# Linear attention and a GELU network on one core: a table of shifts for the order, and three changes of who does what

## The chip, the cores and the metric

The kernel runs on one core of a Trainium2 chip. The metric is the device time of one execution in microseconds (us). Before the change three executions took 814.27 us in the median (813.37 to 816.61). The engines are TensorE (PE in the rows, with PEld for its weight loads), VectorE (DVE), ScalarE (ACT), GpSimd (POOL) and SyncE (SP); DMA transfers are issued by SyncE and GpSimd.

## The reference

q, k and v have 8 batches, 8 heads, 576 positions and 64 channels. The network has 4608 tokens (8 x 576), 512 channels in and out and 2048 hidden ones.

```python
q_s = exp(q - max(q, axis=-1)); q_s = q_s / (sum(q_s, axis=-1) + 1e-9)
k_s = exp(k - max(k, axis=2));  k_s = k_s / (sum(k_s, axis=2) + 1e-9)
kv = einsum('bhsd,bhse->bhde', k_s, v)
x = einsum('bhsd,bhde->bhse', q_s, kv).transpose(0, 2, 1, 3).reshape(4608, 512)
h = x @ w_in
out = (h * (1.0 / (1.0 + exp(-1.702 * h)))) @ w_out
```

So q is normalised over its channels, k over the positions, and each is 64 wide.

## The kernel before

The 4608 tokens are nine blocks t = 0 to 8 of 512. For each block the attention gives x (512 channels by 512 tokens), and the network runs over it in eight steps, each with a pair of 128-wide slices of the hidden layer. The weights arrive as pairs of 32-bit words (float64); `conv` turns them, on ScalarE (L349, L391) and VectorE (L354, L358, L394), into a high and a low part, and every product of the network is taken in three matmuls: high by high, high by low, low by high.

Block 0 multiplies plainly: `plain1` (L895) and `ffn2` (L1200), matmuls of 512 columns. From block 1 the first product, and from block 3 the second as well, is done on half blocks in seven products in place of eight (`ffn1`, `ffn2s`, all through `matmul`, L316, 256 columns, in sixes). These need sums of the weight quarters: `sums` makes those of `w_in` during block 1 (VectorE L462 to L475 and, last, L486 into a tile `wt`, of which there are two), and `sums2` those of `w_out` during block 2 (VectorE L510 to L526, ScalarE L531). The weights and sums go to DRAM (`kept`, `kept_t`, `kept_u`) and are loaded again for every later block, by GpSimd (L426, and `load_u` at L1015).

`sums2` works with two buffers of 4 KB a partition: the finest part `fine` lies in the second half of the tile X (even steps) or in O (odd steps), the rounded part `split` always in the first half of X. Both are stored by SyncE (L529) into interleaved rows: each partition writes four pieces of 1 KB, and `load_u` reads rows of 2 KB.

The attention of block t runs beside the network of block t - 1. For k: maximum over the positions (VectorE, then an all-reduce on GpSimd, L638), subtraction (VectorE L649, L652), exponential (ScalarE L655, L656), and `kv_pairs` on TensorE (L728). For the first batch the subtraction of k is done by TensorE instead (`k_sub_first`, L675 to L680: identity times k plus minus one times the maximum), for all four pairs of heads (hp 0 to 3). For q: `q_soft` takes the maximum (L759), subtracts (L760), takes the exponential on ScalarE (L763), sums (L766), adds 1e-9 (L767), inverts (L768) and multiplies (L769), in one instruction each for a tile of 512 elements a partition; `q_tr` transposes a pair of heads by four small matmuls (L784) and copies them from PSUM (L788); `x_pairs` (L806) multiplies by kv.

After each stretch of such other work on TensorE, `again()` sets a counter: the next BACK matmuls of 256 columns run with their columns reversed, and the STEPS = 4 after them in another permutation. Until the first real work TensorE runs fills on zeros (L302).

The order is not written out by hand. `Plan.add` lists every operation with engine, cost in us, what it reads and writes, and a rank. `due()` goes over TensorE's operations in rank order, adds up their costs and works backwards to the time by which each operation must be done. `forward()` then plays the program: on every engine that is free it starts, among the operations whose inputs are there, the one due first. TABLE is a cost for changing ScalarE's function table, LAND and RATE are costs of a transfer. `order()` gives the instructions of each engine in the order in which the play began them, and they are issued so.

## Time and profile before

| what | value |
|---|---|
| median of three executions | 814.27 us (813.37 to 816.61) |
| the profiled execution | 812.7 us, span 810.9 us, so 1.8 us outside the span |
| TensorE busy | 800.1 us, 99% of the span, 6652 matmuls |
| of these, matmuls of 256 columns at L316 | 4704 (784 sixes) |
| VectorE, ScalarE, GpSimd busy | 679.1, 588.2, 255.9 us |
| granted clock of TensorE | 0.999 of 2.4 GHz |
| DMA | 204.08 MB; SyncE's queue 31.3%, GpSimd's 52.9% of 16 engines |

The span is the time from the first to the last instruction in the trace; the execution's own time is a little longer. A busy share is an average over the whole run. In the order of time, VectorE is nearly full in the first 200 us and has room later. A view in order of time gives the start of a group of like instructions, the time from its first start to its last end, and in brackets idle time ahead of it and who ended it. Matmuls overlap, so that the next group may start before this time is over.

### The profile page before, as it was taken

How to read it: one execution, taken by the hardware profiler on the slowest of the kernel's cores; microseconds unless marked ns; L12 is line 12 of the kernel's file. 1: busy time of each engine (PE TensorE's matmuls, PEld its weight loads, DVE VectorE, ACT ScalarE, POOL GpSimd, SP SyncE). 2: the span in 40 equal slices, each digit the busy share in tenths (PEclk: the TensorE clock that was granted, in tenths of full speed). 3: DMA queues.
4: the chain of work that ended last, by engine and by line, in shares of the span. 5: the costliest groups of instructions: out<-in, count | busy, mean ns of one | idle time of the engine just before them, and what ended most of it. 6: DMA issues, size and time to landing. Idle time of an engine off the chain costs nothing.

```text
span 810.9 us, 17790 instructions
## 1 busy us (share of the span) xinstructions
PE 800.1 (99%) x6652; PEld 736.8 (91%) x6652; DVE 679.1 (84%) x1300; ACT 588.2 (73%) x1136; POOL 255.9 (32%) x439
## 2 busy tenths in 40 slices
PE   9999999999999999999999999999999999999997
PEld 4777789988898879999999999999999999999997
DVE  8999999999869975889779988899889975686557
ACT  5798886887947866896768895899697845565442
POOL 1120202122222442544244423453343234333530
PEclk9999999999999999999999999999999999999999
DMA  9999766776299968997599868986897589768973
GB/s 286 352 355 325 253 234 221 217 246 214 82 331 283 361 204 239 323 317 226 171 272 353 250 183 241 347 275 181 242 298 217 155 246 291 221 170 245 312 229 100
DMA packets 119478, 204.08 MB, mean 252 GB/s; under 512 B 18656, under 2 KB 64224, under 8 KB 118368
## 3 DMA queue, kind: packets, MB, share of 16 engines
q0 software_dynamic: 53856, 123.23, 52.9%
q1 hardware_dynamic: 65536, 79.71, 31.3%
q8 instruction: 53, 0.87, 0.5%
q14 instruction: 33, 0.27, 0.1%
HBM read 168.30 MB, written 34.60 MB: 250 GB/s over the span
## 4 chain that ended last, share of the span: by engine, by line
PE 87%; DMA 6%; DVE 5%; issue 2%; POOL 0%; ACT 0%; SPq 0%; DVEq 0%; POOLq 0%
PE bank L316 64%; PE bank L1200 11%; PE bank L895 3%; PE bank L728 2%; PE bank L806 2%; DMA kept_u<-O 2%; PE bank L784 2%; DMA vl<-in_v 1%; DMA raw<-in_moe_w_out 1%; DMA wj<-kept 1%; DMA raw<-in_moe_w_in 1%; PE bank L302 1%; DMA qT<-in_v 1%; PE bank L675 0%; DVE xo L874 0%
## 5 line engine op out<-in xcount | busy, mean ns | idle before, releaser
L316 PE MATMUL bank<-xo,wt 128*128 128x256 f32 x1536 | 219.4, 278 | 0.5 <-DVE X L964 0.4
L316 PEld LDWEIGHTS bank<-xo,wt 128*128 128x128 f32 x1536 | 198.4, 188 | 9.1 <-issue 1.4
L316 PE MATMUL bank<-xo,wj 128*128 128x256 f32 x1152 | 167.2, 281 | 1.8 <-DVE X L964 1.7
L316 PEld LDWEIGHTS bank<-xo,wj 128*128 128x128 f32 x1152 | 146.8, 188 | 6.4 <-ACT X L970 2.8
L426 POOL DMA_DIRECT2D wj<-kept x138 | 73.2, 531 | 214.9 <-PE bank L316 184.1
L316 PE MATMUL bank<-w,gh 128*128 128x256 f32 x1008 | 140.0, 277 | 0.2
L316 PE MATMUL bank<-w,gl 128*128 128x256 f32 x1008 | 139.2, 277 | 0.0
L964 DVE TENSOR_TENSOR X<-bank,X 128x256 f32<-128x256 f32 x192 | 79.7, 419 | 65.3 <-PE bank L316 53.3
L316 PEld LDWEIGHTS bank<-w,gh 128*128 128x128 f32 x1008 | 126.3, 188 | 0.7 <-issue 0.3
L316 PEld LDWEIGHTS bank<-w,gl 128*128 128x128 f32 x1008 | 126.2, 188 | 0.0
L1200 PE MATMUL bank<-w,gh 128*128 128x512 f32 x384 | 119.8, 393 | 0.8 <-DVE w L394 0.8
L1015 POOL DMA_DIRECT2D w<-kept_u x152 | 80.5, 530 | 119.4 <-PE bank L316 91.5
L960 ACT COPY X<-bank 128x256 f32<-128x256 f32 x192 | 70.1, 370 | 62.4 <-PE bank L316 60.1
L970 ACT ACTIVATE X<-X 128x256 f32<-128x256 f32 x192 | 77.7, 415 | 51.9 <-DVE X L964 51.0
L1124 DVE TENSOR_TENSOR O<-bank,O 128x512 f32<-128x512 f32 x101 | 69.0, 684 | 11.1 <-PE bank L316 10.7
L1200 PEld LDWEIGHTS bank<-w,gh 128*128 128x128 f32 x384 | 66.9, 188 | 12.5 <-DVE w L394 1.3
L1200 PE MATMUL bank<-w,gl 128*128 128x512 f32 x192 | 75.5, 393 | 0.1
L426 POOL DMA_DIRECT2D wt<-kept_t x84 | 44.5, 530 | 83.0 <-PE bank L316 69.3
L1051 DVE TENSOR_TENSOR X<-X 128x512 f32<-128x512 f32 x96 | 66.5, 699 | 4.4 <-ACT X L970 3.2
L638 POOL PARTITION_ALL_REDUCE mx<-mx x32 | 36.7, 1147 | 98.0 <-DVE mx L634 94.6
L1062 DVE TENSOR_TENSOR gh<-X,gh 128x512 fp32r<-128x512 f32 x84 | 57.3, 683 | 8.4 <-ACT gh L1066 8.2
L1062 DVE TENSOR_TENSOR gl<-X,gl 128x512 fp32r<-128x512 f32 x84 | 57.3, 684 | 3.6 <-ACT gl L1066 3.4
(130 smaller groups left out, 1192.1 us busy)
## 6 DMA issues: line engine op xcount, KB each, us to landing
wt<-kept_t POOLq DMA_DIRECT2D x84, 512.0 KB, 5.9
w<-kept_u POOLq DMA_DIRECT2D x152, 256.0 KB, 5.6
wj<-kept POOLq DMA_DIRECT2D x126, 256.0 KB, 5.2
kt<-in_k SPq DMA_DIRECT2D x32, 256.0 KB, 7.0
raw<-in_moe_w_in SPq DMA_DIRECT2D x16, 512.0 KB, 8.4
raw<-in_moe_w_out SPq DMA_DIRECT2D x16, 512.0 KB, 6.6
kept<-wj SPq DMA_DIRECT2D x16, 512.0 KB, 5.7
kept_t<-wt SPq DMA_DIRECT2D x8, 1024.0 KB, 5.0
```

Source lines behind the costliest of these rows:

```text
L316: nc.tensor.matmul(out, w, x, skip_group_check=True, **flags)
L426: "POOL", 0.6, (key,), to, R(t, step - 2, off), lambda: nc.gpsimd.dma_start(out=out(), in_=src), size=size
L638: nc.gpsimd.partition_all_reduce(flat, flat, P, bass_isa.ReduceOp.max)
L895: nc.tensor.matmul(bank[bk], w[:, c // 2, l, c % 2 * P : (c % 2 + 1) * P], x[:, r], start=c == 0 and e == 0, stop=c == KC - 1 and e == 2)
L960: vec("ACT", act(HT), (("bank", bk),), (A(n),), slot, lambda: nc.scalar.copy(a(n), ph[bk]))
L964: nc.vector.tensor_tensor(out=a(n), in0=ph[bk], in1=a(n), op=ALU.add)
L970: vec("ACT", act(HT), K, (A(n),), slot, lambda: nc.scalar.activation(a(n), x, AF.Gelu_apprx_sigmoid), "gelu")
L1015: nc.gpsimd.dma_start(out=wo[s, 0][:, 1].rearrange("p s f -> p (s f)"), in_=kept_u[p][:, c * DM : (c + 1) * DM])
L1051: nc.vector.tensor_tensor(out=x[:, :, o], in0=x[:, :, n], in1=x[:, :, m], op=op)
L1062: nc.vector.tensor_tensor(out=L[s][:, 1], in0=x[:, :, src], in1=L[s][:, 0].bitcast(F32), op=ALU.subtract)
L1124: nc.vector.tensor_tensor(out=half(u, to), in0=bv(b), in1=o, op=ALU.add)
L1200: nc.tensor.matmul(bank[c].rearrange("p (d f) -> p d f", d=2), l, r, start=first_ and e == 0, stop=last and e == 2)
```

## The change

Four things change.

1. The order. A table MOVES of 1535 whole numbers, of which 1263 are not zero, is added, in tenths of a microsecond, to the due times before `forward()` plays the program. The play's constants change: LAND 1.8 to 3.2, RATE 340e3 to 320e3, a TensorE stop of over 1 us after 35 us costs 1.5 more, consecutive instructions overlap by 0.1 us on ScalarE and 0.08 on VectorE, the units of the network on TensorE cost 0.69.
2. First k and q. Of the first k, head pairs 2 and 3 are subtracted by VectorE and go to ScalarE as in later batches; pairs 0 and 1 stay on TensorE. For q of block 0 the maximum is taken negated, and ScalarE takes eight exponentials per tile, each of 64 elements with the maximum as its bias and its sum as a second output (`accum_out`); VectorE's subtraction and its sum go.
3. Transposes. From block 1 `q_tr` does two pairs of head pairs in one run, eight matmuls into two banks. BACK is 5 in place of 6.
4. Sums of `w_out`. In odd steps both parts lie in O; in even steps in X. Each part is stored in one row of 4 KB a partition, and `load_u` reads two pieces of 1 KB.

```diff
--- before.py
+++ after.py
@@ -16,6 +16,57 @@
 AX = mybir.AxisListType
 
 
+MOVES = """
+305 60 -68 -35 0 -21 -48 -501 -1307 -8 -258 14 12 22 44 -23 5 60 -5 -401 45 -45 275 -139 -314 -265 355 -297 20 19 -110
...
+"""
+
+
 class Plan:
 
 
@@ -24,11 +75,13 @@
 
 
 
-    HOP, LAND, RATE, ISSUE = 0.1, 1.8, 340e3, 0.5
+    HOP, LAND, RATE, ISSUE = 0.1, 3.2, 320e3, 0.5
     AHEAD = 6.0
+    STALL = 1.5
 
     WARM = 27.0
     TABLE = {"ACT": 1.28, "POOL": 7.0}
+    OVERLAP = {"ACT": 0.1, "DVE": 0.08}
 
     def __init__(self):
         self.ops, self.fill = [], None
@@ -94,7 +147,10 @@
                 _, cost, _, _, _, needs, size, late = ops[n]
                 if needs is not None and needs != table.get(e):
                     cost, table[e] = cost + self.TABLE[e], needs
-                free[e] = done = now + cost
+                if e == "PE" and now > 35.0 and now - free[e] > 1.0:
+                    cost += self.STALL
+                done = now + cost
+                free[e] = done - self.OVERLAP.get(e, 0.0)
                 if size:
                     wire = max(wire, done) + size / self.RATE
                     done = wire + self.LAND + late
@@ -116,12 +172,16 @@
                 now = min(times)
         return began, start, end
 
+    def moved(self, due):
+        moves = [0.1 * int(x) for x in MOVES.split()]
+        return [min(d, 1e6) + (moves[n] if n < len(moves) else 0.0) for n, d in enumerate(due)]
+
     def order(self):
         self.users = [[] for _ in self.ops]
         for n, o in enumerate(self.ops):
             for d in o[2]:
                 self.users[d].append(n)
-        began, self.start, self.end = self.forward(self.due())
+        began, self.start, self.end = self.forward(self.moved(self.due()))
         return began
 
 
@@ -210,6 +270,7 @@
     mx = [sb(f"mx{i}", [P, 2, D]) for i in range(NP)]
     m1 = sb("m1", [P, 2, 2, D])
     qm = [sb(f"qm{i}", [P, 2 * C]) for i in range(2)]
+    qs_ = [X[1][:, 1, 0, 8 * i : 8 * i + 8] for i in range(2)]
     r_ = sb("r", [P, 2, NP])
     rs = [r_[:, i] for i in range(2)]
     kl, vl = sb("kl", [P, H, D]), sb("vl", [P, H, W])
@@ -303,7 +364,7 @@
 
     plan.fill = 0.3, fill
 
-    BACK, STEPS = 6, 4
+    BACK, STEPS = 5, 4
     odd = [BACK + STEPS]
 
     def matmul(out, w, x, **flags):
@@ -499,11 +560,12 @@
     def sums2(step, rank):
 
         p = NS - 1 - step
-        split, H = X[1][:, 0, 0:4], [("X", 1, 0, n) for n in range(4)]
         if step % 2:
-            fine, K = O[1].rearrange("p u (d f) -> p (u d) f", d=2), [("O", 1, n // 2, n % 2) for n in range(4)]
+            split, fine = (y.rearrange("p u (d f) -> p (u d) f", d=2) for y in O)
+            H, K = [("tmp", n) for n in range(2)], [("O", 1, n // 2, n % 2) for n in range(4)]
         else:
-            fine, K = X[1][:, 1, 0:4], [("X", 1, 1, n) for n in range(4)]
+            split, fine = (X[1][:, y, 0:4] for y in range(2))
+            H, K = ([("X", 1, y, n) for n in range(4)] for y in range(2))
 
         def run_f(jj):
             x = wo[p, jj].bitcast(F32)
@@ -526,7 +588,7 @@
             nc.vector.tensor_tensor(out=fine, in0=fine, in1=split, op=ALU.subtract)
 
         def run_s(y, x):
-            nc.sync.dma_start(out=kept_u[p].rearrange("p (i s f) -> p s i f", i=4, s=2)[:, y], in_=x)
+            nc.sync.dma_start(out=kept_u[p][:, 2 * y * DM : 2 * (y + 1) * DM], in_=x.rearrange("p i f -> p (i f)"))
 
         plan.add("ACT", act(4 * HT), K, H, rank, lambda: nc.scalar.copy(split.bitcast(F32R), fine))
         plan.add("SP", plan.ISSUE, H, (("kept_u", p, 0),), rank, lambda: run_s(0, split), size=2 * DM * P * 4, late=2.0)
@@ -656,7 +718,7 @@
             nc.scalar.activation(kl[0:ST, hs], kl[0:ST, hs], AF.Exp)
 
         K, L = ("kt", hp), ("kl", hp)
-        if b == 0:
+        if b == 0 and hp in (0, 1):
             k_sub_first(hp, rank)
             return
         plan.add("DVE", dve(2 * CM * D) + dve(2 * D), (K, M, "kl"), (K, L), rank, run)
@@ -749,6 +811,7 @@
 
     def q_soft(t, hp, rank):
         m, M = qm[hp % 2].rearrange("p (c h) -> p c h", c=C), ("qm", hp % 2)
+        bias = t == 0 and hp in (0, 1, 2, 3)
         x, K, held = qt[hp], ("qt", hp), ()
         if t == 0:
             x, (K, *held) = early_tile("q", hp)
@@ -756,36 +819,57 @@
         qx, Q = q_ready(t, hp)
 
         def run_m():
-            nc.vector.tensor_reduce(out=m, in_=x, axis=AX.X, op=ALU.max)
-            nc.vector.tensor_tensor(out=x, in0=x, in1=bc(m, D), op=ALU.subtract)
+            nc.vector.tensor_reduce(out=m, in_=x, axis=AX.X, op=ALU.max, negate=bias)
+            if not bias:
+                nc.vector.tensor_tensor(out=x, in0=x, in1=bc(m, D), op=ALU.subtract)
 
         def run_e():
-            nc.scalar.activation(x, x, AF.Exp)
+            if not bias:
+                nc.scalar.activation(x, x, AF.Exp)
+                return
+            for c in range(C):
+                for h in range(2):
+                    nc.scalar.activation(
+                        x[:, c, h], x[:, c, h], AF.Exp, bias=m[:, c, h : h + 1], accum_out=sums_[:, c, h : h + 1]
+                    )
 
         def run_s():
-            nc.vector.tensor_reduce(out=m, in_=x, axis=AX.X, op=ALU.add)
-            nc.vector.tensor_scalar_add(m, m, 1e-9)
+            if not bias:
+                nc.vector.tensor_reduce(out=m, in_=x, axis=AX.X, op=ALU.add)
+            nc.vector.tensor_scalar_add(m, sums_ if bias else m, 1e-9)
             nc.vector.reciprocal(m, m)
             nc.vector.tensor_tensor(out=qx.rearrange("p c (h d) -> p c h d", h=2), in0=x, in1=bc(m, D), op=ALU.mult)
 
         e = 2 * C * D
+        sums_ = qs_[hp % 2].rearrange("p (c h) -> p c h", c=C)
+        if bias:
+            SM_ = ("qs", hp % 2)
+            plan.add("DVE", dve(e), (K,), (M,), rank, run_m)
+            plan.add("ACT", 8 * 0.25, (K, M), (K, SM_), rank, run_e, table="exp")
+            plan.add("DVE", dve(e) + 0.45, (K, SM_, *held), (Q, M), rank, run_s)
+            return
         plan.add("DVE", 2 * dve(e), (K,), (K, M), rank, run_m)
         plan.add("ACT", act(e), (K,), (K,), rank, run_e, table="exp")
         plan.add("DVE", 2 * dve(e) + 0.45, (K, *held), (Q, M), rank, run_s)
 
-    def q_tr(t, hp, rank):
-        bk = next_bank(t)
-        pq = bank[bk]
-        qx, QK = q_ready(t, hp)
+    def q_tr(t, hps, rank):
+        bks = [next_bank(t) for _ in hps]
 
         def run():
             again()
-            for c in range(C):
-                nc.tensor.transpose(pq[:, c * P : (c + 1) * P], qx[:, c], ident)
-
-        PB, Q = ("bank", bk), ("qT", hp % 2)
-        plan.add("PE", 0.45, (QK, "ident"), (PB,), rank, run)
-        plan.add("ACT", act(TB), (PB,), (Q,), rank, lambda: nc.scalar.copy(qT[hp % 2], pq))
+            for hp, bk in zip(hps, bks):
+                qx = q_ready(t, hp)[0]
+                for c in range(C):
+                    nc.tensor.transpose(bank[bk][:, c * P : (c + 1) * P], qx[:, c], ident)
+
+        PBs = [("bank", bk) for bk in bks]
+        plan.add("PE", 0.45 * len(hps), [*(q_ready(t, hp)[1] for hp in hps), "ident"], PBs, rank, run)
+        for hp, bk, PB in zip(hps, bks, PBs):
+
+            def run_c(hp=hp, bk=bk):
+                nc.scalar.copy(qT[hp % 2], bank[bk])
+
+            plan.add("ACT", act(TB), (PB,), (("qT", hp % 2),), rank, run_c)
 
     def x_pairs(t, half, rank):
         hps = (2 * half, 2 * half + 1)
...
@@ -1013,7 +1097,7 @@
 
         def run():
             nc.gpsimd.dma_start(
-                out=wo[s, 0][:, 1].rearrange("p s f -> p (s f)"), in_=kept_u[p][:, c * DM : (c + 1) * DM]
+                out=wo[s, 0][:, 1], in_=kept_u[p].rearrange("p (s i f) -> p s i f", s=2, i=4)[:, :, c]
             )
 
         plan.add("POOL", 0.6, [("kept_u", p, y) for y in range(2)], (("wb", s), *more), rank, run, size=DM * 4 * P)
...
@@ -1238,7 +1322,10 @@
                 at(n(far + 1.7 + 0.3 * hp), load_v, t, hp)
             at(n(far + 1.5 + 0.3 * hp), load_q, t, hp)
             at(n(2.7 + 0.05 * hp if t else 1.3 + 0.8 * hp), q_soft, t, hp)
-            at(n((3.0, 3.3, 4.6, 4.9)[hp]), q_tr, t, hp)
+            if t == 0:
+                at(n((3.0, 3.3, 4.6, 4.9)[hp]), q_tr, t, (hp,))
+            elif hp % 2:
+                at(n((0, 3.3, 0, 4.9)[hp]), q_tr, t, (hp - 1, hp))
         if new:
             if t == 0:
                 for half in range(2):
...
```

TensorE, from the third first-k block of before on (kt and kl are tiles of k, mx their maxima, vl and kl the last positions; earlywo holds v). Before:

```order
L675 MATMUL bank2_65<-kt2_84,ident_71 128x512
L676 MATMUL bank2_65<-mx2_98,X1_75 128x512
L677 MATMUL bank6_69<-kl_104,ident_71 64x128
L680 MATMUL bank6_69<-mx2_98,X1_75 64x128
L675 MATMUL bank3_66<-kt3_85,ident_71 128x512
L676 MATMUL bank3_66<-mx3_99,X1_75 128x512
L677 MATMUL bank6_69<-kl_104,ident_71 64x128
L680 MATMUL bank6_69<-mx3_99,X1_75 64x128
L728 MATMUL bank1_64<-earlywo60_146,kt0_82 64x64 x8
L728 MATMUL bank1_64<-vl_105,kl_104 64x64 x2
L728 MATMUL bank1_64<-vl_105,kt0_82 64x1 x8
L728 MATMUL bank1_64<-vl_105,kl_104 64x1 x2
```

After, from the second first-k block on (X0 on L363 is the tile of zeros, qt0 and qt1 are q):

```order
L737 MATMUL bank1_64<-kt1_83,ident_71 128x512
L738 MATMUL bank1_64<-mx1_97,X1_75 128x512
L739 MATMUL bank4_67<-kl_104,ident_71 64x128
L742 MATMUL bank4_67<-mx1_97,X1_75 64x128
L363 LDWEIGHTS X0_74
L363 MATMUL bank5_68<-X0_74 128x512
L863 MATMUL bank6_69<-ident_71,qt1_91 128x128 x4
L363 LDWEIGHTS X0_74
L363 MATMUL bank5_68<-X0_74 128x512
L363 LDWEIGHTS X0_74
L363 MATMUL bank5_68<-X0_74 128x512
L863 MATMUL bank3_66<-ident_71,qt0_90 128x128 x4
```

The last two blocks of k are gone from TensorE, and two runs of transposes of q stand where they were, ahead of kv; six more fills stand ahead of the first of all (25 in place of 19).

VectorE, the end of the fourth weight sum of block 1 (wt0 is the sum's low part; qt, qm and kt are the next block's q). Before:

```order
L759 TENSOR_REDUCE qm1_102<-qt1_91 128x8
L760 TENSOR_TENSOR qt1_91<-qt1_91,qm1_102 128x4x2x64
L766 TENSOR_REDUCE qm0_101<-qt0_90 128x8
L767 TENSOR_SCALAR qm0_101<-qm0_101 128x8
L768 RECIPROCAL qm0_101<-qm0_101 128x8
L769 TENSOR_TENSOR kt0_82<-qt0_90,qm0_101 128x512
L964 TENSOR_TENSOR X0_74<-bank5_68,X0_74 128x256
L486 TENSOR_TENSOR wt0_1397<-X1_75,wt0_1397 128x4x256
L766 TENSOR_REDUCE qm1_102<-qt1_91 128x8
```

After, the same sum at L547:

```order
L838 TENSOR_REDUCE qm1_102<-qt3_93 128x8
L839 TENSOR_SCALAR qm1_102<-qm1_102 128x8
L840 RECIPROCAL qm1_102<-qm1_102 128x8
L841 TENSOR_TENSOR kt3_85<-qt3_93,qm1_102 128x512
L536 TENSOR_TENSOR X1_75<-X1_75 128x512
L822 TENSOR_REDUCE qm0_101<-qt2_92 128x8
L824 TENSOR_TENSOR qt2_92<-qt2_92,qm0_101 128x4x2x64
L1063 TENSOR_TENSOR gl0_78<-X0_74,gh0_76 128x2x256
L1048 TENSOR_TENSOR X0_74<-bank5_68,X0_74 128x256
L547 TENSOR_TENSOR wt0_1396<-X1_75,wt0_1396 128x4x256
```

The end of q's fourth tile, the beginning of its third and a split of the hidden values (L1063) have moved ahead of the sum, which was the 294th row and is the 311th.

TensorE, the transposes of the first two tiles of q in a block, in the middle of the network's sixes (kt0 and kt1 hold the normalised q; bank6 and bank7 take the result). Before, beside block 2:

```order
L784 MATMUL bank6_69<-ident_71,kt0_82 128x128 x4
L316 MATMUL bank4_67<-xo8_1161,wj10_108 128x256 x6
L316 MATMUL bank5_68<-xo9_1258,wt1_111 128x8x2x16 x4
L316 MATMUL bank5_68<-xo9_1258,wt1_111 128x256 x2
L1200 MATMUL bank0_63<-w_764,gh0_76 128x512 x2
L1200 MATMUL bank0_63<-w_764,gl0_78 128x512
L1200 MATMUL bank0_63<-w_830,gh0_76 128x512 x2
L1200 MATMUL bank0_63<-w_830,gl0_78 128x512
L1200 MATMUL bank1_64<-w_764,gh0_76 128x512 x2
L1200 MATMUL bank1_64<-w_764,gl0_78 128x512
L316 MATMUL bank4_67<-xo10_1304,wt1_111 128x256 x6
L784 MATMUL bank7_70<-ident_71,kt1_83 128x128 x4
```

After, beside the same block:

```order
L377 MATMUL bank5_68<-xo6_1380,wj00_106 128x256 x6
L863 MATMUL bank6_69<-ident_71,kt0_82 128x128 x4
L863 MATMUL bank7_70<-ident_71,kt1_83 128x128 x4
L377 MATMUL bank4_67<-xo7_1369,wt0_1396 128x256 x5
L377 MATMUL bank4_67<-xo7_1369,wt0_1396 128x8x2x16
L377 MATMUL bank5_68<-xo9_1185,wt1_111 128x8x2x16 x3
L377 MATMUL bank5_68<-xo9_1185,wt1_111 128x256 x3
```

The two runs stood apart, each with turned matmuls behind it, and now follow one another, with five reversed matmuls behind both.

## Rows read from the trace of the kernel before

**Rows 1.** Busy times by stage: length, busy per engine, clock, DMA share

```profile
23.00:60.00 37.00, 35.87 (x236) 26.88 (x235) 35.67 (x71) 31.98 (x56) 7.20 (x8) 1.00 1.06 353
60.00:100.00 40.00, 39.24 (x201) 30.23 (x200) 37.95 (x77) 34.69 (x59) 4.98 (x4) 1.00 0.95 300
100.00:150.00 50.00, 50.00 (x324) 43.55 (x324) 48.11 (x89) 37.78 (x70) 7.27 (x9) 1.00 0.61 211
```

**Rows 2.** TensorE in order of time: start, us, line, operation, count, idle before

```profile
207.35 0.87 PE L316 MATMUL bank<-xo,wt 128*128 128x256 f32 x6
208.30 0.97 PE L316 MATMUL bank<-xo,wj 128*128 128x256 f32 x6
...
287.13 0.87 PE L316 MATMUL bank<-xo,wt 128*128 128x256 f32 x6
289.67 0.97 PE L316 MATMUL bank<-xo,wj 128*128 128x256 f32 x6 [1.67 <-DVE X L964]
...
381.00 0.84 PE L316 MATMUL bank<-xo,wj 128*128 128x256 f32 x6
382.20 0.97 PE L316 MATMUL bank<-xo,wt 128*128 128x256 f32 x6 [0.36 <-DVE X L964]
```

**Rows 3.** The chain of waits between 270 and 292 us: start, us, what

```profile
275.55 13.01 DMA kept_u<-O
```

**Rows 4.** VectorE in order of time

```profile
153.33 1.22 DVE L486 TENSOR_TENSOR wt<-X,wt 128x1024 fp32r<-128x1024 f32 x1
154.46 0.68 DVE L766 TENSOR_REDUCE qm<-qt 128x8 f32<-128x512 f32 x1
...
288.58 0.69 DVE L510 TENSOR_TENSOR O<-w 128x512 f32<-128x512 f32 x1 [1.14 <-DMA kept_u<-O]
```

**Rows 5.** TensorE in order of time, the fourth sum's first use

```profile
154.72 0.96 PE L316 MATMUL bank<-xo,wt 128*128 128x256 f32 x6
```

**Rows 6.** Instructions grouped by line and form: busy us, mean ns, idle before

```profile
L760 DVE TENSOR_TENSOR qt<-qt,qm 128x512 f32<-128x512 f32 x32 | 22.1, 692 | 1.1
...
L742 ACT ACTIVATE kvn<-bank,r 128x64 f32<-128x64 f32 x32 | 7.6, 322 | 1.7 <-DVE r L734 1.7
...
L768 DVE RECIPROCAL qm<-qm 128x8 f32<-128x8 f32 x36 | 7.3, 203 | 1.2
```

**Rows 7.** TensorE in order of time, at a run of transposes

```profile
419.76 0.85 PE L316 MATMUL bank<-xo,wt 128*128 128x256 f32 x6
420.45 0.60 PE L784 MATMUL bank<-ident,kt 128*128 128x128 f32 x4
...
421.61 0.85 PE L316 MATMUL bank<-xo,wj 128*128 128x256 f32 x6
```

**Rows 8.** VectorE's waits between 23 and 190 us: total, times, longest

```profile
DVE X L964 <- PE bank L316: 1.7, 3, 0.8
```

**Rows 9.** The chain of waits in the first 30 us

```profile
1.24 5.78 PE bank L302 x19
...
17.37 2.28 PE bank L728 x70
```

**Rows 10.** The page's list of DMA issues: count, KB each, us to landing

```profile
kept_u<-O SPq DMA_DIRECT2D x4, 512.0 KB, 8.1
```

**Rows 11.** ScalarE in order of time

```profile
293.75 1.04 ACT L531 CAST X<-O 128x1024 fp32r<-128x1024 f32 x1
...
306.79 0.60 ACT L1210 COPY O<-bank 128x512 f32<-128x512 f32 x1
```

**Rows 12.** DMA queues between 8 and 30 us: packets, MB, share

```profile
q1 hardware_dynamic: 8001, 7.21, 108.5%
```

**Rows 13.** DMA queues and issues between 400 and 484 us

```profile
q0 software_dynamic: 7820, 17.37, 71.7%
q1 hardware_dynamic: 5136, 4.46, 20.1%
...
w<-kept_u POOLq DMA_DIRECT2D x24, 256.0 KB, 7.2
```

8 lines of the change are left out of this document (4 added, 4 removed), and 46 rows, old and new, of the table MOVES.

## Prediction

> **What bounds the kernel now.** I read the busy times by stage first. TensorE works 50.00 of 50 us between 100 and 150 and stands still for 1.9 us in the 77 us before [rows 1]. So the end moves only where TensorE stands, or where its own work gets shorter or slower. In the same rows VectorE works 35.67 of 37, 37.95 of 40 and 48.11 of 50 us: it has 5.3 us of idle time in 127. Until the weight sums of block 1 are made, VectorE is nearly as full as TensorE, and what its order puts ahead of those sums decides when TensorE gets them.
>
> Next I read TensorE in order of time for its stops. The largest lies between the six matmuls at 287.13, which at the usual pace are through in 0.7 us, and those at 289.67: 1.83 us lost [rows 2]. The one after 381.00 loses 0.52 (382.20 less 381.00, less 0.68). Four small ones, 0.95 us together, lie between 191 and 208.3; the last of them is 0.26 (208.30 less 207.35, less 0.69). What stands still before 100 us lies ahead of the sums. The chain of waits says what the large one is: a store of `kept_u` out of O takes 13.01 us to land, VectorE's next sum into O waits for it, and an addition into X that TensorE waits for stands behind that sum on VectorE [rows 3, 4].
>
> Last, the fourth weight sum: VectorE makes it at 153.33, taking 1.22 us [rows 4], and the first matmuls that read it start at 154.72 [rows 5]. It comes just in time, 0.2 us early.
>
> **The change part by part.**
>
> *VectorE ahead of the sums.* From the first weight conversion to the fourth sum, the new order has 20 instructions more on VectorE: two maxima and two subtractions of q, two sums and two products of q, one split of the hidden values and three passes of 512 elements for the sums of `w_out` (twelve of 512 elements in all, at 0.69 us or a little less [rows 6]: 8.2 us), two passes of half that size (0.8), and six small ones at 0.2 us or less (1.1): 10.1 us. Each instruction begins before the one before it has ended (153.33 + 1.22 is 154.55, the next begins at 154.46 [rows 4]); I take 0.04 us each off, 0.9. VectorE's first conversion comes about 0.6 us earlier (next part). TensorE's own order puts 3.0 us more in front of that use: six matmuls of 256 columns (0.69, from 419.76 to 420.45 [rows 7]), six of 512 (twice that), one run of transposes (0.5) and four matmuls of x (0.5). Less the 0.2 us of room: 10.1 - 0.9 - 0.6 - 3.0 - 0.2 = 5.4 us late, if VectorE idles as long as before. By the same count the first sum would be 2.9 us late, the second 1.8, the third 3.6 and the sixth, where VectorE is 11.7 us behind and TensorE only 0.5, some 6.2. These are not added, since a wait at one sum shifts all that follows; the upper end is +6.2. If VectorE had no idle time the fourth sum would be about 0.1 late; that is the lower end, +0.1, since nothing that TensorE gains before 155 us outlives a wait for this sum. Of the idle 5.3 us only 1.7 is a wait for TensorE, in three pieces [rows 8], which a VectorE that runs behind would not have; the rest is spread thinly. I take +3.0, the middle. TensorE's 1.9 us of standing before 100 are inside this number.
>
> *The start.* Two of the four first k's leave TensorE. The four take from 7.02, where the 19 fills end, to 17.37 [rows 9], 2.59 each, so 5.2 us go; six more fills of 0.30 (5.78 over 19) come back, and two runs of transposes stand ahead of kv. TensorE alone would be some 1.7 us earlier at the end of kv. But ScalarE gets two more plain exponentials and, for each q tile, eight small ones in place of one. An Exp of 64 elements with an accumulated sum isn't in the trace; between the 0.20 us of VectorE's reciprocal of 8 elements and the 0.32 of ScalarE's product of 64 [rows 6], a tile is 1.6 to 2.6 us (2.6 taken, the nearest in kind), and two of the four tiles stand ahead of what TensorE needs. So the start of block 0 lies between 2 us earlier and 1.5 later; I take 0.4 earlier for TensorE and 0.6 for VectorE. Both are already spent in the fourth sum. The four subtractions and four sums that leave VectorE (5.5 us) stand before or around the first conversions and are in the count above.
>
> *Stores of the sums of w_out.* They become rows of 4 KB, and odd steps use O for both parts. The sum that waited for its own store at 288 still has about as many instructions before it in VectorE's new order (18 where it had 19), so it goes only if the store lands sooner. The four stores out of O land in 8.1 us by the median [rows 10], and the sum could have gone on 11.9 us after the issue (288.58 less its wait of 1.14 [rows 4], less 275.55). With 13.01 it stays, 1.83; with anything under 11.9 it goes. I take -1.8. What is late next there is the addition into X, by nothing I can see. The change adds a wait: O's first half is now also read by a store, and block 2's output copies on ScalarE and VectorE, with the additions into X behind them, must find it landed. The last cast is at 293.75, so the store leaves near 294.8 and lands near 302.9; the first copy was at 306.79 [rows 11]. It is covered by 3.9 us.
>
> *Loads of those sums.* Each of 152 loads becomes 256 packets of 1 KB in place of 128 of 2 KB. On SyncE's queue a packet of 0.90 KB took 47.7 ns (108.5% of 16 engines over 22 us, 8001 packets [rows 12]), on GpSimd's one of 2.2 KB 123 ns (71.7% over 84 us, 7820 packets [rows 13]): by bytes two small ones cost what one large one does, so 0; if a packet cost 123 ns at any size, 123 ns more per pair. Cover: GpSimd's loads land several us before their use, and the engines are busy at 0.92 of their time between 400 and 484 (0.717 for GpSimd's queue, 0.201 for SyncE's [rows 13]). I take 0.
>
> The Trainium skill, "DMA: Bandwidth & Descriptors" (Why small descriptors are slow), speaks against this part: it states a fixed overhead of about three cycles a packet, on beats of 32 bytes. By it 2 x 35 cycles stand against 67, an estimate of 4.5% more for these loads, or about one point of the share of 0.92. The sum would stay as it is; it makes the fourth rival below no likelier than I have it, and no run here shows it yet.
>
> *Transposes of two pairs in one run,* 16 times: now a run of four and the six matmuls behind it take 1.16 us (420.45 to 421.61), an undisturbed six 0.69 [rows 7]. Half of the 0.47 is the transposes themselves; one turn less saves 0.01 to 0.06 each: -0.5. *Five reversed matmuls rather than six* after each of some 70 turns, about 0.005 each: -0.3 (bounds -0.6 and 0, apart from the fifth rival).
>
> *The table's other moves.* The stop at 381 goes with the order (-0.5, bounds -0.5 and 0), and the four before 208 too (-0.9, bounds -0.95 and 0), since the instructions around them change places. From block 3 to the end TensorE's order is almost the same, and I take nothing there.
>
> **The sum:** +3.0 - 1.8 - 0.5 - 0.3 - 0.5 - 0.9 = -1.0 on the profiled execution's 812.7 (span 810.9 and 1.8 outside it), 811.7. The median of the runs shown is 1.6 above that execution, so 813.3. With all bounds low: 0.1 - 1.83 - 0.9 - 0.6 - 0.5 - 0.95 = -4.7, 809.6; all high: +6.2, 820.5.
>
> **The rivals.**
> *Second:* VectorE fills its idle time, the sums come as before, and every later stop goes, the sum with all bounds low: 809.6. For it: the stops are short and have one releaser each. Against: 3.6 of VectorE's 5.3 us idle has no named cause, and the sums must come at the very first moment that they can.
> *Third:* VectorE idles as before and the later stops come back in other places: +6.2 - 0.8, 819.7. For it: VectorE's 11.7 us at the sixth sum. Against: a queue that is never empty should idle less.
> *Fourth, on the slower side:* loads in 1 KB rows fill the DMA engines in blocks 3 to 8. Between 400 and 484 there is room from 0.92 to the 1.08 seen when full [rows 12]: 0.16 x 16 x 84 = 215 us of engine time for 24 x 128 = 3072 more packets [rows 13], so it decides from 70 ns a packet. At 80 ns each such stretch is 1.9 us longer, and 152 loads are 6.3 such stretches: +12, 825. For it: nothing but the bound of 123. Against: both measured packets go by bytes.
> *Fifth, slower too:* sixes of matmuls of 256 columns have a slower pace in some stretches, 0.87 from first start to last end at 207.35 and 287.13 [rows 2] against 0.85 at 419.76 [rows 7]. If five reversed ones don't end such a stretch where six did, half of the 784 sixes slower by 0.02 is +8, 821.
>
> **How the numbers follow.** Half a per cent, 4.1 us, is about what a measurement can tell from no change. Chances: forecast 0.47 (its own range 810.3 to 818), second 0.32, third 0.10, fourth 0.06, fifth 0.05. The second takes in times below 809.6 where the slower pace gets rarer (a hundred sixes are 2 us). So faster 0.32, same 0.47, slower 0.21, and the range 806.5 to 820.
>
> **What would show it.** Right: TensorE stops for some us in all before a weight sum between 115 and 185 us, the releaser named being VectorE's sum or its neighbours; VectorE's idle time between 23 and 150 below 4 us; no stop over 1 us near 288; `kept_u` stores landing under 10 us; share between 400 and 484 still near 0.92. Wrong: no stop at the sums, TensorE's start off by over 2 us, a share over 1.0 after 400, waits of matmuls for `w`, or sixes at the slower pace over long stretches.

## The result and the profile after

The changed kernel takes 819.87 us in the median (819.75 to 820.07, 4 runs) against 813.96 (813.37 to 816.61, 4 runs) for the kernel before on the same chip: 1.0065 times as long [1.0046, 1.0083]. It is slower by 5.9 us; I had forecast 813.3, no change. The profiled execution has a span of 817.9 us, 7.0 more than before. The kernel before spreads from 811.5 to 820.6 us over the executions on a single chip, the four of the changed one lie within 0.3; why is open, and a ratio to before is known to some 0.2 to 0.3%.

The busy times by stage of the changed kernel (columns as in [rows 1]: length, PE, PEld, DVE, ACT, POOL, clock, DMA share, GB/s):

```profile
23.00:60.00 37.00, 34.36 (x149) 24.37 (x148) 34.48 (x70) 31.45 (x60) 13.34 (x8) 0.95 0.99 326
60.00:100.00 40.00, 39.88 (x271) 30.82 (x270) 36.75 (x72) 35.43 (x60) 0.68 (x1) 1.00 0.95 296
100.00:150.00 50.00, 48.35 (x274) 39.52 (x274) 48.44 (x94) 42.48 (x72) 12.27 (x11) 1.00 0.62 207
...
200.00:300.00 100.00, 100.00 (x718) 88.24 (x717) 80.14 (x152) 70.43 (x137) 27.66 (x44) 1.00 0.83 259
```

TensorE stands for 4.4 us of the 127 between 23 and 150 (before 1.9), and VectorE idles 7.3 us there (before 5.3). Between 200 and 300 TensorE now works throughout. TensorE's stops in order of time in the changed kernel (L1284 is the plain second product, L377 the sixes, in brackets the idle time before a group and who ended it):

```profile
41.19 0.39 PE L1284 MATMUL bank<-w,gh 128*128 128x512 f32 x1
43.34 0.50 PE L1284 MATMUL bank<-w,gh 128*128 128x512 f32 x1 [1.76 <-DVE w L455]
...
44.97 1.06 PE L1284 MATMUL bank<-w,gh 128*128 128x512 f32 x2
45.83 0.63 PE L1284 MATMUL bank<-w,gl 128*128 128x512 f32 x1
...
124.14 0.50 PE L1284 MATMUL bank<-w,gh 128*128 128x512 f32 x1 [0.91 <-DVE w L455]
...
138.28 0.97 PE L377 MATMUL bank<-xo,wt 128*128 128x256 f32 x6 [0.36 <-DVE X L1048]
...
166.19 0.98 PE L377 MATMUL bank<-xo,wt 128*128 128x256 f32 x6
...
470.43 0.95 PE L377 MATMUL bank<-w,gl 128*128 128x256 f32 x6 [0.71 <-DVE O L1208]
...
555.13 0.97 PE L377 MATMUL bank<-w,gl 128*128 128x256 f32 x6 [0.70 <-DVE O L1208]
```

The stops of [rows 2] at 287 and 381 are gone. New is one of 1.92 us (43.34 less 41.19, less 0.23) at the first use of the weights `w_out`: TensorE waits for VectorE's low part of them (`w` from L455). Two matmuls of 512 columns take 0.86 us behind it (45.83 less 44.97), 0.43 each, where 0.23 is usual. The granted clock (the column before the DMA share) is 0.50 there, the lower of its two levels, 1.2 GHz:

```profile
44.50:47.60 3.10, 3.10 (x9) 2.34 (x7) 2.50 (x5) 2.74 (x5) 2.47 (x3) 0.50 1.08 374
```

About 2 us go there. The wait at 124 is for the same line. Two stops of about 0.86 at 470 and 555 are new too. The first use of the fourth weight sum, at 166.19, has no wait ahead of it, though it comes 11.5 us later than in [rows 5].

The fourth weight sum on VectorE ends at 164.77, 10.2 later than in [rows 4]:

```profile
163.56 1.21 DVE L547 TENSOR_TENSOR wt<-X,wt 128x1024 fp32r<-128x1024 f32 x1
164.81 0.69 DVE L523 TENSOR_TENSOR X<-wj 128x512 f32<-128x512 f32 x1
```

VectorE's waits between 23 and 190 us, as in [rows 8], name GpSimd and ScalarE, and no longer TensorE:

```profile
DVE kt L711 <- POOL mx L700: 2.6, 5, 0.6
DVE gl L997 <- ACT gh L1001: 1.6, 1, 1.6
```

The transfers landed no later than forecast. The stores of `kept_u` out of O land in 7.1 us ([rows 10]: 8.1), the loads of it in 5.4 where they took 5.6. Between 400 and 484 there are 3003 packets more on GpSimd's queue than in [rows 13], its share is 0.03 more and SyncE's 0.01 less:

```profile
q0 software_dynamic: 10823, 17.27, 74.7%
q1 hardware_dynamic: 5136, 4.46, 18.9%
...
w<-kept_u POOLq DMA_DIRECT2D x24, 256.0 KB, 7.3
```

To see where the 7 us arise I compared the start of the same matmul of the network in both traces. "Work" is how much of the network's product TensorE has behind it, counted in us at the undisturbed pace; the other rows are the lateness against before, in us (the other work that stands between may be earlier or later by some 2 to 3 us in one order than in the other):

```
work done           0     10     20     40     70     90    130    180    390    705
time in before   27.5   39.0   49.1   75.9  108.1  128.3  173.6  227.5  464.0  800.3
changed kernel   +2.6   +1.3   +5.5   +2.2   +5.1   +6.7  +10.0   +8.3   +6.8   +6.7
both relieved    +2.6   +1.3   +2.2   -0.7   +2.0   +2.1   +4.7   +2.8   +1.5   +1.7
```

The 6.7 are there by 128 us, and what follows adds nothing in the balance. (The last line is an experiment below.)

### The profile page after: what moved, and what is told of

Read it like the earlier page. It is cut to its first block, busy times and chain, and to the rows that moved or that the text cites. A ratio compares the mean times of both kernels' runs of the same rounds, so it can differ in the third digit from the quotient of the medians.

```text
span 817.9 us, 17838 instructions
## 1 busy us (share of the span) xinstructions
PE 804.9 (98%) x6654; PEld 737.0 (90%) x6656; DVE 673.7 (82%) x1296; ACT 576.4 (70%) x1185; POOL 293.4 (36%) x439
## 4 chain that ended last, share of the span: by engine, by line
PE 78%; DVE 10%; DMA 5%; ACT 2%; issue 2%; SPq 1%; POOL 1%; DVEq 0%; ACTq 0%; POOLq 0%
PE bank L377 64%; PE bank L1284 9%; PE bank L790 2%; PE bank L890 2%; PE bank L863 2%; DMA wj<-kept 1%; DMA kt<-in_k 1%; ACT earlywo L832 1%; DMA kl<-in_k 1%; DVE wide L415 1%; DMA kept<-wj 1%; DVE w L455 1%; DMA qT<-in_v 1%; DVE gl L997 1%; POOL mx L700 1%
## 5 line engine op out<-in xcount | busy, mean ns | idle before, releaser
L377 PE MATMUL bank<-xo,wt 128*128 128x256 f32 x1536 | 218.6, 279 | 0.4 <-DVE X L1048 0.4
L377 PEld LDWEIGHTS bank<-xo,wt 128*128 128x128 f32 x1536 | 195.9, 188 | 9.6 <-ACT X L1044 2.4
L377 PE MATMUL bank<-xo,wj 128*128 128x256 f32 x1152 | 164.8, 279 | 0.2
L377 PEld LDWEIGHTS bank<-xo,wj 128*128 128x128 f32 x1152 | 148.0, 188 | 5.2 <-DVE X L1048 1.0
L1099 POOL DMA_DIRECT2D w<-kept_u x152 | 107.9, 710 | 111.0 <-PE bank L377 88.5
L487 POOL DMA_DIRECT2D wj<-kept x138 | 74.9, 542 | 202.2 <-PE bank L377 170.8
L377 PE MATMUL bank<-w,gl 128*128 128x256 f32 x1008 | 140.2, 277 | 1.6 <-DVE O L1208 1.4
L377 PE MATMUL bank<-w,gh 128*128 128x256 f32 x1008 | 140.5, 278 | 0.0
L377 PEld LDWEIGHTS bank<-w,gl 128*128 128x128 f32 x1008 | 126.1, 188 | 2.5 <-DVE O L1208 1.8
L377 PEld LDWEIGHTS bank<-w,gh 128*128 128x128 f32 x1008 | 126.1, 188 | 1.0 <-ACT X L1054 0.3
L1284 PE MATMUL bank<-w,gh 128*128 128x512 f32 x384 | 122.3, 399 | 2.8 <-DVE w L455 2.7
L1284 PEld LDWEIGHTS bank<-w,gh 128*128 128x128 f32 x384 | 67.6, 190 | 15.5 <-DVE w L455 4.3
L1284 PE MATMUL bank<-w,gl 128*128 128x512 f32 x192 | 76.5, 399 | 0.2 <-DVE gl L997 0.2
L700 POOL PARTITION_ALL_REDUCE mx<-mx x32 | 41.3, 1292 | 66.3 <-DVE mx L696 66.0
```

The source lines that it names most:

```text
L377: nc.tensor.matmul(out, w, x, skip_group_check=True, **flags)
L487: "POOL", 0.6, (key,), to, R(t, step - 2, off), lambda: nc.gpsimd.dma_start(out=out(), in_=src), size=size
L700: nc.gpsimd.partition_all_reduce(flat, flat, P, bass_isa.ReduceOp.max)
L1099: nc.gpsimd.dma_start(out=wo[s, 0][:, 1], in_=kept_u[p].rearrange("p (s i f) -> p s i f", s=2, i=4)[:, :, c])
L1284: nc.tensor.matmul(bank[c].rearrange("p (d f) -> p d f", d=2), l, r, start=first_ and e == 0, stop=last and e == 2)
```

## What VectorE does ahead of the stop at 41 us

VectorE in order of time in the changed kernel:

```profile
37.00 0.68 DVE L711 TENSOR_TENSOR kt<-kt,mx 128x512 f32<-128x512 f32 x1
...
40.82 0.69 DVE L711 TENSOR_TENSOR kt<-kt,mx 128x512 f32<-128x512 f32 x1 [0.60 <-POOL mx L700]
41.43 0.28 DVE L714 TENSOR_TENSOR kl<-kl,mx 64x128 f32<-64x128 f32 x1
41.63 0.41 DVE L694 TENSOR_TENSOR m<-kt 128x256 f32<-128x256 f32 x1
...
42.61 0.68 DVE L455 TENSOR_TENSOR w<-wide,w 128x512 fp32r<-128x512 f32 x1
...
45.42 1.07 DVE L711 TENSOR_TENSOR kt<-kt,mx 128x512 f32<-128x512 f32 x1 [0.60 <-POOL mx L700]
...
47.37 0.68 DVE L455 TENSOR_TENSOR w<-wide,w 128x512 fp32r<-128x512 f32 x1
```

and in the kernel before, the same first conversion and the same first subtraction of block 1's k:

```profile
37.61 0.68 DVE L394 TENSOR_TENSOR w<-wide,w 128x512 fp32r<-128x512 f32 x1
...
50.19 1.10 DVE L649 TENSOR_TENSOR kt<-kt,mx 128x512 f32<-128x512 f32 x1
```

The subtraction of k, whose result TensorE first multiplies at 62.07 us (before 56.79), has moved from 50 to 37 us. With its maxima it is ahead of the conversion, and it waits for GpSimd's all-reduce with the conversion behind it. What the conversion needs from ScalarE was there at 40.12, before that wait began:

```profile
39.50 0.62 ACT L452 CAST w<-wide 128x512 fp32r<-128x512 f32 x1
```

So `w` ends at 43.3 where it ended at 38.3.

## The experiments

My theory became (D in the expectations; A had put the loss at the weight sums, B and C at TensorE's own stops and the first transfers): VectorE's order is late at two places, at 33 to 47 us (block 1's k ahead of the first conversions of `w_out`) and at 96 to 138 us (block 2's q and k and the first sums of `w_out` ahead of conversions and weight sums). The rivals: TensorE's own early work and the late start; the small exponentials; the loads in rows of 1 KB; and that VectorE has too much work in any order. An edit that leaves out work keeps the play's costs, so that the order of the rest stays as it is. Runs in the changed order are set against 819.87 us, runs of the kernel before against before on their own chip. The changed kernel itself was timed on one chip only, so differences under 1 us are not certain.

**More of TensorE, more of VectorE.**

```diff
+    twice = c == 0 and 1 <= step <= 4      # plain1, eight matmuls more
...
-    nc.vector.tensor_tensor(out=dst(1), in0=fv, in1=dst(0).bitcast(F32), op=ALU.subtract)
+    for _ in range(2 if kind == "wi" and jj == 0 and 2 <= p <= 4 else 1):
+        nc.vector.tensor_tensor(out=dst(1), in0=fv, in1=dst(0).bitcast(F32), op=ALU.subtract)
```

> The changed kernel (819.9 us) with eight more matmuls of 512 columns on TensorE in steps 1 to 4 of block 0 (the first of each group is issued twice), 8 x 0.229 = 1.8 us of more TensorE work before 100 us. Theory A (VectorE, late and with idle time, sets the pace until the last weight sum of block 1): TensorE has to wait later anyway, so no more than +0.5, 819.9 to 820.4. Theory B (TensorE's own early stop at 41 us and what it loses there sets the end): all of it is paid, +1.8, 821.7.

819.96 (819.68 to 820.36): 1.8 us more on TensorE cost 0.1.

> The changed kernel with three more subtractions of 512 elements on VectorE (the low part of the weights of pairs 2 to 4 is computed twice), 3 x 0.60 = 1.8 us of more VectorE work ahead of the first weight sum. Theory A: VectorE's lateness is paid, less what falls into its own waits, +1.0 to +1.8, 821 to 821.7. Theory B: VectorE is not what counts, -0.2 to +0.4, near 820.

822.31 (822.09 to 822.43): three subtractions more, 1.8 us, cost 2.4 (in its profile 0.55 of that stand already at the first matmul, ahead of the edit). Both are as theory A had it, the second beyond its 821.7. What is early on TensorE is free; VectorE's work at this place is paid in full.

**The parts by themselves.** The first k and q undone in the changed kernel (`if b == 0:`, `bias = False`, each number of the table kept with its operation); the same two put alone into the kernel before; then each of them alone:

> The changed kernel with the sharing of the first k and q undone: all four k on TensorE, q of block 0 subtracted and summed on VectorE with one Exp a tile; the table's numbers stay with their operations. Theory A (ScalarE's 32 small Exps, 2.65 us a tile with the reading of the sum, hold back the first conversions by 1.6 us, and that is carried to the sums): the first conversion on VectorE back near 23.0 us and the time down by 1.5 to 4 us, 816 to 818.4. Rival (the order by the table alone, 20 more instructions of VectorE ahead of the fourth sum, carries the loss): within 1 us of 819.9.

> The kernel before with only the sharing of the first k and q: no table, old constants, transposes and stores. Theory A: ScalarE's start is late by about 1.5 us, and as the fourth sum has 0.2 us of room, +1 to +3, 815 to 817. Rival (the share costs nothing, the order by the table does): within 0.7 us of 814.0.

> The kernel before with only the first k shared (head pairs 2 and 3 on VectorE and ScalarE). The whole share cost 4 to 5 us. If the small Exps of q carry it: within 1 us of before. If the k part does (VectorE gets 2.1 us more, and the order of SyncE's loads moves): +3 or more.

> The kernel before with only q of block 0 by eight small Exps a tile on ScalarE. If the small Exps carry the share's cost (0.33 us each by the trace of the changed kernel, 2.65 us a tile against 0.63, 8 us on ScalarE before 24 us): +3 to +5, 817 to 820. If the k part does: within 1 us of before.

837.72 (837.22 to 838.54), 17.9 more than the changed kernel. Alone in before 819.05 (817.31 to 821.13) against 815.19; k alone 820.83 against 815.51, q alone 822.33 against 815.51. Each half costs more than both together, and neither theory of the first two runs held. The play lists everything anew for every input, so these runs price a new order, not a part; they show only that the first k and q gain nothing without an order that suits them.

**The table.** All its numbers read as zero:

```diff
-        return [min(d, 1e6) + (moves[n] if n < len(moves) else 0.0) for n, d in enumerate(due)]
+        return [min(d, 1e6) + 0.0 for n, d in enumerate(due)]
```

> The changed kernel with every number of the table at 0, all else as changed. If the table's order is what makes VectorE late at the sums: down by 3 to 6 us, 814 to 817. If the table mends what the other parts cost: up by 2 or more, over 822. Theory A with the late start as the main cost: little, within 2 us of 819.9.

824.67 (822.99 to 826.48), 4.8 slower than with it. This too is a new order, but one thing can be read from it. Without the table VectorE also subtracts k of block 1 ahead of the first conversion of `w_out`, three times:

```profile
34.23 0.68 DVE L711 TENSOR_TENSOR kt<-kt,mx 128x512 f32<-128x512 f32 x1
...
42.16 1.27 DVE L455 TENSOR_TENSOR w<-wide,w 128x512 fp32r<-128x512 f32 x2
```

So the early k is not the table's doing. With the first k and q alone in the kernel before, the first such subtraction is at 53.80, behind the conversions. It comes with the play's other constants or the other edits; no run tells these apart.

**One exponential a tile of q,** in the changed kernel's order; the maximum isn't subtracted and the sums of q in block 0 are other numbers:

```diff
-            for c in range(C):
-                for h in range(2):
-                    nc.scalar.activation(
...
+            nc.scalar.activation(x, x, AF.Exp)
+            nc.scalar.copy(sums_, m)
```

> The changed kernel in its own order on all engines, but each of the four q tiles of block 0 takes one Exp of 512 elements and a copy of 8 elements on ScalarE in place of eight Exps of 64 with their reading of sums (left out: the maximum's subtraction and the true sums, so these rows of q are not normalised). ScalarE has 1.9 us less per tile, 7.5 us in all before 24 us. Theory A (the late start of the conversions costs, and VectorE carries it to the sums): the first conversion on VectorE 2 to 3 us earlier and the time down by 2 to 4 us, 816 to 818. Rival (the table's order alone makes VectorE late): within 0.7 us of 819.9.

819.27 (818.38 to 819.7): 0.6. VectorE's first conversion then begins at 23.05 in place of 24.56, yet TensorE waits again for `w`, in two pieces, and with no matmul at half pace between them:

```profile
41.74 0.50 PE L1281 MATMUL bank<-w,gh 128*128 128x512 f32 x1 [1.33 <-DVE w L455]
...
46.49 0.50 PE L1281 MATMUL bank<-w,gh 128*128 128x512 f32 x1 [1.73 <-DVE w L455]
```

So the late start costs little, and the slow clock is not the cause: where the clock stays up, the second conversion is waited for instead. The next run shows this again. It does the same work as the changed kernel until 280 us, has no slow clock, stands for 1.7 us before 43.48 and 1.9 before 48.24, and is only 0.1 us behind the changed kernel after 20 us of work.

**Loads in rows of 2 KB** (from wrong places of `kept_u`), **and the fourth part of the change alone in the kernel before** (stores, buffers and loads of the sums):

```diff
-  out=wo[s, 0][:, 1], in_=kept_u[p].rearrange("p (s i f) -> p s i f", s=2, i=4)[:, :, c]
+  out=wo[s, 0][:, 1].rearrange("p s f -> p (s f)"), in_=kept_u[p][:, c * DM : (c + 1) * DM]
```

> The changed kernel in its own order, but the 152 loads of the sums of w_out read rows of 2 KB as before (from where the other layout had them, so these products are not those of the reference). GpSimd's issue should fall from 0.71 to 0.53 us each. Theory A: no change before 300 us and next to none after, 819.2 to 820.1. Rival (loads in 1 KB rows are late from block 3 on and make the new stops at 469 and 554 us): down by 1 to 2, 818 to 819.

> The kernel before with only the new stores, buffers and loads of the sums of w_out. The prediction's term: the stop at 288 us goes, -1.8, 812 to 813. If the store lands as late as before: 814 +/- 0.7. Loads in 1 KB rows as a cost: over 815.

821.1 (820.78 to 821.43), so the larger rows are not faster, as neither theory had it; the 1.2 are lost between 468 and 590 us, why stays open. They do cost the DMA engines less. Between 400 and 484 the share of GpSimd's queue is 0.697, where it is 0.747 in the changed kernel with its 1 KB rows:

```profile
q0 software_dynamic: 7773, 17.30, 69.7%
```

The fourth part alone: 815.9 against 815.7, ratio 1.0002 [0.9975, 1.0029]. That is a gain and a loss. The stop at 288 is gone, but at 238 TensorE stands 3.57 us, since ScalarE's cast, which now writes O, waits for a store of the output out of O (TensorE, then ScalarE):

```profile
238.41 0.98 PE L316 MATMUL bank<-xo,wj 128*128 128x256 f32 x6 [3.57 <-ACT X L971]
...
237.03 1.04 ACT L532 CAST O<-O 128x1024 fp32r<-128x1024 f32 x1 [4.04 <-DMA out<-O]
```

So this run doesn't price the 1 KB rows by themselves.

**Less work for VectorE in block 1's q** (50 to 90 us): its 16 passes, 8 us, work on 2 of 64 columns, in the changed kernel and in the one before:

```diff
+    w = 2 if t == 1 else D
-    nc.vector.tensor_reduce(out=m, in_=x, axis=AX.X, op=ALU.max, negate=bias)
+    nc.vector.tensor_reduce(out=m, in_=x[:, :, :, 0:w], axis=AX.X, op=ALU.max, negate=bias)
```

> The changed kernel in its own order, with VectorE relieved: the sixteen passes over q of block 1 (maximum, subtraction, sum and product of four tiles, all during block 0) take 16 elements a partition rather than 512, so that x of block 1 is not the reference's. 16 x 0.5 = 8 us less on VectorE ahead of the first weight sum. Theory A (VectorE's lateness at the sums is the loss): TensorE is late there by some 10 us against the kernel before, of which 1.3 to 2.6 is its own start; down by 5 to 8 us, 812 to 815. Theory C (the transfers of the first 60 us or TensorE's own stops are the loss): down by less than 2, over 818.

> The same relief of 8 us of VectorE in the kernel before (x of block 1 is not the reference's there either). Theory A: before was in balance, with 0.2 us of room at the fourth sum and 1.9 us of stops before 100 us; down by 1 to 2.5 us against before, and so within 2 us of the changed kernel with the same relief. Theory C: the two relieved kernels stay 4 to 6 us apart.

818.88 (818.52 to 819.25), 1.0 less; before 815.06 against 815.51, ratio 0.9988 [0.9962, 1.0014]. Of 8 us hardly one arrives, which is far from the 5 to 8 of theory A. VectorE's waits between 23 and 190 us in the relieved changed kernel say why (total, times, longest):

```profile
DVE gl L999 <- ACT gh L1003: 4.6, 3, 1.6
...
DVE w L455 <- ACT w L452: 2.3, 4, 0.8
...
DVE wj L455 <- ACT wj L452: 0.7, 3, 0.3
```

With less work of its own VectorE stands and waits for ScalarE's half of the conversions and splits: between 60 and 100 us it idles 8.8 us, where it idled 3.3.

**The two places relieved:** k of block 1 on 2 of 64 columns (the 20 passes at 33 to 47 us); q and k of block 2 and the first two sums of `w_out` on fewer columns (96 to 138 us); both:

```diff
-    nc.vector.tensor_tensor(out=m1, in0=t[:, :, 0:2], in1=t[:, :, 2:4], op=ALU.max)
+    w = 2 if b in (1, 2) else D
+    nc.vector.tensor_tensor(out=m1[..., 0:w], in0=t[:, :, 0:2, 0:w], in1=t[:, :, 2:4, 0:w], op=ALU.max)
...
+    f = 16 if step < 2 else HT
+    nc.vector.tensor_tensor(out=fine[:, o, 0:f], in0=fine[:, x, 0:f], in1=fine[:, y, 0:f], op=ALU.subtract)
```

> The changed kernel in its own order, with VectorE relieved between 33 and 47 us: the twenty passes over k of block 1 (three for each maximum, two for each subtraction) take 2 of 64 columns, so that kv of the second batch is not the reference's. Theory D (two places where VectorE's order makes TensorE wait: the first conversions of w_out behind k of block 1 at 41 to 47 us, and VectorE's unbroken work from 96 to 138 us): the stop at 41 us and the slow clock behind it go, 4 us of TensorE, but the second place takes part of it back: down by 1 to 3, 817 to 819. Theory C (the transfers of the first 60 us are the loss): within 0.7 of 819.9.

> The changed kernel in its own order, with VectorE relieved between 96 and 138 us: the passes over q and k of block 2 take 2 of 64 columns and those of the first two sums of w_out 16 of 256 (all but the two that write O first); some 4 us less there. Theory D: TensorE's stops between 86 and 138 us, 3.0 us in all, go: down by 2 to 3.5, 816.4 to 818. Theory C: within 0.7 of 819.9.

> Both reliefs at once in the changed kernel's own order. Theory D: both places gone, down by 5 to 7, 813 to 815, level with the kernel before. Theory C, or a loss spread over the whole program: over 817.

816.99 (816.34 to 817.84), 817.57 (816.56 to 818.27) and 814.05 (813.49 to 815.11): 2.9, 2.3 and 5.8 less than the changed kernel, the last 0.9976 of before [0.9959, 0.9993]. Each is about what theory D had expected, and the two add up. The busy times by stage with both relieved:

```profile
23.00:60.00 37.00, 36.41 (x201) 25.90 (x201) 32.96 (x74) 33.56 (x63) 6.62 (x8) 1.00 1.00 325
60.00:100.00 40.00, 39.55 (x238) 30.52 (x235) 36.73 (x73) 35.64 (x62) 1.89 (x2) 1.00 0.99 329
100.00:150.00 50.00, 49.48 (x335) 42.41 (x334) 44.85 (x106) 41.12 (x73) 7.21 (x10) 1.00 0.65 213
```

and its TensorE at the first use of `w_out`:

```profile
43.91 0.39 PE L1291 MATMUL bank<-w,gh 128*128 128x512 f32 x1
44.50 0.50 PE L1291 MATMUL bank<-w,gh 128*128 128x512 f32 x1 [0.21 <-DVE w L455]
```

Of the wait for `w` 0.21 is left, and TensorE stands 1.6 us between 23 and 150. The start is as late as in the changed kernel (+2.6 in the table above).

**The same reliefs in the kernel before,** to tell the place of the work from its amount:

> The kernel before with the first of the two reliefs: the 20 passes of VectorE for block 1's k (maxima and subtractions) work on 2 of 64 columns, the order as it is; k of that block is wrong. In the changed kernel the same relief gave 2.9 us. If the two places are late because of where the new order puts this work (ahead of the first conversions of w_out), before, whose order makes these subtractions only after those conversions, gains little: -1.0 to 0, 814.5 to 815.5. If VectorE's amount of work is what counts, wherever it stands, before gains as much, -2.5 or more: under 813.

> The kernel before with both reliefs: k of blocks 1 and 2, q of block 2, and the first two sums of w_out on fewer columns, the order as it is; these parts of k, q and the sums are wrong. In the changed kernel both together gave 5.8 us. Order theory: before gains at most 2, 813.5 to 815.5, and stays level with the changed kernel relieved in the same way (814.05) or above it. Amount theory: before gains some 5 to 6, 809.5 to 810.5, and the changed kernel stays that much behind when both are relieved.

815.04 (814.01 to 817.52) and 816.21 (813.91 to 819.52) against 815.38: ratios 0.9985 [0.9966, 1.0005] and 1.0001 [0.9981, 1.0021]. The passes whose loss gives the changed kernel 5.8 us are worth nothing in the order before, to within some 1.7 us. It is their place.

**A version that should have been better:** the changed kernel, computing all of the reference, with two waits for the play to heed.

```diff
+   first = (("conv", "wo", 0, 1),) if b == 1 else ()            # k of block 1 after w_out's first pair
+   plan.add("DVE", dve(2 * CM * D) + dve(2 * D), (K, M, "kl", *first), (K, L), rank, run)
...
+   (f"wo{p}{jj}", *((("sum", 5),) if step < 3 else ()))          # first sums of w_out after the sixth weight sum
```

> The changed kernel with the table, but with two more dependencies for the play: k of block 1 is subtracted after the first pair of w_out is converted, and the first three sums of w_out start after the sixth weight sum of block 1. The whole computation is kept. Theory D: the two places shrink, down by 2 to 5, 815 to 818. If the list changes elsewhere at random: anything from 815 to 830.

841.29 (838.96 to 842.22), 21 slower, outside both ranges. The subtraction of k did move behind the first conversions (these begin at 41.87 and 45.03, it at 45.97), but passes over q came ahead of them in its place, and TensorE still waits 1.54 us for `w` at 43. The play listed all else anew; TensorE stands 5.2 us between 23 and 60, 5.0 between 100 and 150 and 5.5 between 150 and 200:

```profile
23.00:60.00 37.00, 31.84 (x139) 22.13 (x137) 35.73 (x73) 34.57 (x62) 7.88 (x8) 0.95 1.02 334
...
100.00:150.00 50.00, 44.97 (x281) 35.51 (x282) 44.22 (x87) 41.28 (x69) 19.75 (x10) 1.00 0.49 169
150.00:200.00 50.00, 44.47 (x289) 37.02 (x289) 41.55 (x79) 40.91 (x69) 12.95 (x16) 1.00 0.68 209
```

## Why the prediction was wrong

*VectorE ahead of the sums, +3.0.* This is the step that failed. The direction was right, the size and the place were not. In place of 3.0 the two reliefs give back 5.8, and TensorE is 6.7 us late by 128 us. Of the 11.5 by which the first use of the fourth sum comes later, some 3.5 is work that TensorE's order puts ahead of it (I had 3.0; the run of x takes 1.0, not 0.5), and the rest is lateness that it brings along. I let the count begin at the first weight conversion and end at a sum, and asked only whether TensorE would have to wait for that sum. It does not: it is already late, because it waited earlier, at the conversions of `w_out` (1.92 and 1.08 us). I had waved the stops before 100 us through as lying inside the number. The middle between 0.1 and 6.2 rested on VectorE idling less once its queue was never empty; it idles 2.0 more, since the order gives it instructions whose inputs come from GpSimd and ScalarE (2.6 and 1.6). VectorE's own lateness of 10.2 at the fourth sum can be taken apart by its rows from the first conversion to that sum, before and after (DVE is the third busy time):

```profile
22.99:153.33 130.34, 128.45 (x796) 103.69 (x795) 124.87 (x241) 107.73 (x187) 19.97 (x22) 1.00 0.83 275
24.56:163.56 139.00, 135.11 (x813) 106.79 (x812) 131.83 (x260) 117.12 (x201) 27.34 (x22) 0.99 0.82 263
```

It starts 1.6 later (I had 0.6 earlier), works 7.0 more (I had 10.1 less 0.9) and idles 1.7 more (I had between none and 5.3 less). Of the signs that I had named for being wrong, three came: no stop at the sums, a start off by over 2 us, and waits for `w`.

*The start, -0.4 and -0.6.* It came out the wrong way: the first matmul is 2.6 late, 1.3 after 10 us of work, and VectorE's first conversion begins at 24.56, 1.6 later than before. The small exponentials take 2.65 us a tile, as I had taken them, but ScalarE has 32 of them until 23.4, and its first conversion waits behind them to 23.56 (before 15.90). I counted two tiles ahead of what TensorE needs; what VectorE needs stands behind all four. Its worth is small, some 0.6 by the run with one exponential.

*The stop at 288, -1.8, the one at 381, -0.5, and the small ones near 200, -0.9.* Right for the first two: both are gone. At 192.7, 197.3 and 200 to 208 some 0.6 of 0.95 is left. But 1.7 us came back at 470 and 555, which I did not see. There VectorE again has a subtraction of k that waits for GpSimd ahead of a sum that TensorE waits for:

```profile
468.47 0.69 DVE L711 TENSOR_TENSOR kt<-kt,mx 128x512 f32<-128x512 f32 x1 [0.61 <-POOL mx L700]
469.08 0.70 DVE L714 TENSOR_TENSOR kl<-kl,mx 64x128 f32<-64x128 f32 x1
469.70 0.67 DVE L1208 TENSOR_TENSOR O<-bank,O 128x512 f32<-128x512 f32 x1
```

That is argued from the trace; no run took it away.

*Transposes and turns, -0.5 and -0.3.* Not told apart by a run. The lateness falls from 8.3 at 227 us to 6.7 at the end, and by the busy times by stage TensorE stands 0.8 less than before between 200 and 800, so some 0.8 may be theirs. The traces fit that: after 160 us a run of four transposes with the ten matmuls of 256 columns behind it takes 1.62 us before (median of 23), a run of eight with ten such matmuls 2.05 after (median of 11). With 1.15 for ten undisturbed, an estimate of 0.04 saved a pair, 0.6 in sixteen.

*Loads and stores, 0.* The share between 400 and 484 is 0.94, under the 1.08 seen when full, and loads land no later, so 0 fits the time, though no run prices it alone. The reason was wrong: two small packets cost more than a large one. The 0.747 against 0.697 above, for the same 17.3 MB, is 67 us of engine time (0.05 x 16 x 84), 22 ns for each of 3072 pairs (24 loads of 128), well under the 70 from which the fourth rival would have decided. The Trainium skill, "DMA: Bandwidth & Descriptors" (Why small descriptors are slow), would have had these loads about 4.5% dearer by an estimate from its figure. The trace shows more: they are 36% of the bytes, and by their part of the 0.697 an estimate of some 20%.

*The rivals.* The third, VectorE idling as before and the later stops coming back elsewhere, gave 819.7. It is the nearest in kind, but VectorE idles more than before, not as before, and the loss stands at the first use of `w_out` rather than at the sums; that its size fits so well is partly luck. I gave it 0.10 because a queue that is never empty should idle less. The wait at 40.82 shows the flaw: VectorE stood for 0.60 us on a subtraction of k while the conversion behind it had its input from ScalarE. That the range to 820 just holds the time is luck too, since its upper end stood for a wait at the sums.
